# Block transposes on VectorE and a trip through DRAM in place of TensorE transposes, in a gated linear attention followed by a feed-forward layer

## The chip, the cores and the metric

The kernel runs on one core of one Trainium2 chip. A core has a matrix engine (TensorE, PE in the profile), three engines for elementwise work (VectorE or DVE, ScalarE or ACT, GpSimd or POOL) and SyncE (SP), which here issues nearly all DMA transfers. Each engine has a queue of instructions of its own, which it works through in order, and they wait for each other by semaphores. The metric is the device time of one execution in microseconds (us), lower is better.

## What is computed

Two layers. The first is a recurrence with a complex gate for each of 4 batches and 8 heads, over 768 steps, with head size 48. The second is a feed-forward layer over all 3072 tokens, 384 to 2048 to 384.

```python
mag = np.sqrt(a_re * a_re + a_im * a_im)
scale = np.minimum(mag, 0.999) / (mag + 1e-06)
a_re_n, a_im_n = (a_re * scale, a_im * scale)
for t in range(S):
    new_re = ar * S_re - ai * S_im
    new_im = ar * S_im + ai * S_re
    S_re, S_im = (new_re + k[t] outer v[t], new_im)
    y[:, :, t] = q[t] @ S_re
x = y.transpose(0, 2, 1, 3).reshape(B * S, H * D)
h = x @ w_in
sp = np.maximum(h, 0.0) + np.log1p(np.exp(-np.abs(h)))
out = (h * erf(sp)) @ w_out
```

Activations are float32; the two weight matrices come in as 64-bit words and are narrowed in the kernel.

## The kernel before

**Units and chunks.** The 3072 tokens are cut into 12 units of 256 tokens, three units to a batch; a unit has two chunks of 128 tokens. The recurrence is done a chunk at a time: gates are turned into a decay `pr` and an angle (cosine and sine, `CS`), keys and queries are multiplied with both, and then a chunk is a masked product of queries and keys, plus the contribution of the state S that the chunks before have left.

**The steps of a chunk** (function `chunk`, lines 981 to 1067), in order:

- `prep` (L977, L992), VectorE: `kr` or `qr` = key or query times decay, then `kt` or `qt` = that times cosine and sine. `kt` and `qt` have 128 tokens as partitions and 8 heads x 96 numbers along the row.
- `cols` (L1001, L1004): the score product needs the 96 numbers as partitions, so TensorE transposes `kt` and `qt` head by head into PSUM (4 heads to a tile `tr`, 4 tiles a chunk), and ScalarE or VectorE copies each tile into `kT` or `qT`. Keys are copied by ScalarE; the queries by ScalarE before unit 3 and by VectorE from unit 3 on (`qact` in `WHEN`); the very first chunk does it the other way about for keys.
- `state` (L1024, L1033, L1035): `kt` times `v`, added to the old state, times the decay over the chunk (`w`, a row of `pr` that goes to DRAM and comes back as a column, L967 and L970).
- `scores` (L1012, L1015): for each head `kT` as weights, `qT` as columns; VectorE multiplies with the triangle and leaves `A`.
- `xT` (L1060, L1064): `A` with `v`, and `qT` with the state, in blocks of 32 output partitions, into one PSUM tile; ScalarE copies it into `xT`. The first chunk of a batch has no part with the state.

A float32 product is two matmul instructions in the profile, a transpose is one.

**The feed-forward part.** `ff_in` (L1080, L1082) multiplies `xT` with `w_in`, eight row blocks of 128 to a slab, two slabs a unit. `softplus` and `erf_times_h` (L726, L1108 to L1111) put each slab through ScalarE and VectorE. `ff_out_8` (L1140) and, for units 3 to 10, `ff_out_7` (L1178, with sums on VectorE at L1125, L1126, L1192, L1195) multiply with `w_out`; the result leaves by L1150 and L1211.

**Order.** Every step of every unit has a place on one line of time, counted in units: the table `WHEN` and lines 1300 to 1342. All steps are sorted by it (L1360), and a scheduling layer turns this order into the queues of the engines. A chunk's steps stand at its begin plus the offsets `st`. Gates of a unit are done well ahead (`gr`, or `gate` for units 2 and 3): `g_mag`, `g_tan`, `g_log`, `g_turn`, `g_angle`, `g_decay`, `g_sin`. Keys, queries and values of a unit are loaded 0.38 units ahead (L1325).

**Waits on transfers.** SP's queue holds loads, the decay rows, output stores and, in `g_angle` from unit 3 on, a row that carries the angle from one chunk to the next (L931), for which VectorE waits at L932. Each issue waits in SP's order.

**Buffers.** `kt`, `qt`, `z` and `yy` have one buffer, `kT` two, `qT` three. `T["s"]`, `T["y"]` are scratch tiles of the gates, `lr` the log of the decay; the row of L931 lands in `s`.

Of the kernel before, what the change touches and what calls it, by code (L numbers as in the profile page):

```python
# [10 lines left out]
FP = mybir.dt.float32  # L11
# [5 lines left out]
OP = mybir.AluOpType  # L17
PSUM = bass.MemoryType.PSUM

P = 128  # L20
# [15 lines left out]
def weave(*streams):  # L36
# [5 lines left out]
    for _, _, _, step in sorted(order, key=lambda e: e[:3]):  # L42
# [1 line left out]

WHEN = {'qact': 3,
 'a00': [0.385, 0.699, 0.3, 0.31, 0.32, 0.33, 0.569, 0.34, 0.35, 0.63],
 'a01': [0.526, 0.422, 0.611, 0.637, 0.649, 0.542, 0.659, 0.66, 0.67, 0.681],
 'n': [0.676, 0.782, 0.769, 0.972, 1.105, 1.183, 1.312, 1.472, 1.61, 1.914, 1.96, 2.139, 2.151, 2.632, 2.395],  # L50
 'g1': [0.702, 0.752, 0.792, 0.802, 0.835, 0.842, 0.873],
 'att': {1: [[0.931, 1.297], 1.089], 2: [[1.716, 2.133], 1.029], 3: [[3.038, 3.627], 1.205]},
 'gate': {2: [1.212, 1.259, 1.372, 1.391, 1.423, 1.442, 1.362], 3: [1.508, 1.606, 1.912, 2.106, 2.59, 2.234, 2.172]},
 'hps': {0: [[0.767, 0.876], [1.01, 1.426]],
         1: [[1.778, 2.017], [2.342, 2.684]],
         2: [[3.136, 3.262], [3.538, 3.868]],
         11: [[11.97, 12.371], [12.438, 12.72]]},
 'act': {0: [2.6, 2.924],
         1: [3.328, 3.7],
         2: [4.148, 4.4],  # L60
         3: [4.9, 5.2],
         4: [5.752, 6.098],
         10: [11.679, 12.031],
         11: [12.456, 12.882]},
 'ops': {0: [3.021, 3.377, 3.704],
         1: [4.001, 4.639, 4.84],
         2: [4.452, 4.798, 4.884],
# [1 line left out]
         10: [12.146, 12.41, 13.01],  # L69
         11: [12.97, 13.469, 14.216]},  # L70
 'T': 5.125,
 'gr': [-1.569, -1.419, -1.119, -0.953, -0.478, -0.129, -1.279],
 'st': [0.014, 0.03, 0.059, 0.09, 0.12, 0.15, 0.206, 0.25, 0.281, 0.388],
 'hr': [1.113, 1.509, 1.573, 1.938],
 'ar': [1.472, 1.947],
 'or': [2.163, 2.683, 3.173],
# [4 lines left out]
 'rest': 12.3,  # L81
 'ok': 13.7,
 'al': [[11.145, 11.515], [11.266, 11.738]],
 'qone': 0,
 'c1g': [0.36, 0.37, 0.38],
 'warm': 0.335}

# [526 lines left out]
def quotient_path(  # L614
# [62 lines left out]
    make_identity(nc, ident)  # L677
    triu = const.tile([P, P], FP, name="triu")
    make_upper_triangular(nc, triu, val=1.0, diag=True)
    cold = tmp.tile([P, P], FP, tag="m", name="cold")  # L680
    vector.memset(cold, 0.0)
    ones = const.tile([P, 1], FP, name="ones")
    vector.memset(ones, 1.0)
# [193 lines left out]
    def g_(nm, u, cc):  # L877
        if cc[0] == 0:
            T[nm, u] = gat.tile([P, C, DM], FP, tag=nm, name=nm)
        return T[nm, u][:, cc[0]:cc[1]]  # L880
# [4 lines left out]
    def g_mag(u, cc=ALL):  # L885

        ar, ai = gate(u, cc)
        s, y = t_("s", cc), t_("y", cc)
        T["s", u] = T["s"]
        i = u * C + cc[0]  # L890
        T["kept"] = u == 1
        act(out=s, in_=ar, func=AF.Square, accum_out=large[:, i:i + 1])
        act(out=y, in_=ai, func=AF.Square)
        T["kept"] = False
        vector.tensor_tensor(out=s, in0=s, in1=y, op=OP.add)
# [14 lines left out]
    def g_log(u, cc=ALL):  # L910
        s, y = T["s"][:, cc[0]:cc[1]], T["y"][:, cc[0]:cc[1]]
        act(out=s, in_=s, func=AF.Ln)
        act(out=y, in_=s, func=AF.Exp, scale=-0.5)
        act(out=y, in_=y, func=AF.Ln, scale=EPS, bias=1.0)
        vector.tensor_scalar(out=s, in0=s, scalar1=0.5, scalar2=math.log(CAP), op0=OP.mult, op1=OP.min)
        T["logs"] = vector.tensor_tensor(out=g_("lr", u, cc), in0=s, in1=y, op=OP.subtract)

    def g_turn(u, cc=ALL):
        th = T["th", u][:, cc[0]:cc[1]]
# [2 lines left out]
    def g_angle(u, c):  # L922

        th = T["th", u][:, c, :]
        goes_on = u % PER > 0 or c > 0
        on_pe = u < PER
        if goes_on:
            prev = T["F", u][:, c - 1, :] if c > 0 else T["F", u - 1][:, C - 1, :]
            if not on_pe:
                row = T["s", u][0:1, c, :]  # L930
                nc.sync.dma_start(out=row, in_=prev[P - 1:P, :])  # L931
                vector.scalar_tensor_tensor(out=th[0:1, :], in0=row, scalar=TAU, in1=th[0:1, :],  # L932
                                               op0=OP.mult, op1=OP.add)
        ps = ps_b.tile([P, DM], FP, tag="b", name="sum")
        nc.tensor.matmul(out=ps, lhsT=turns, rhs=th, start=True, stop=not (goes_on and on_pe))
        if goes_on and on_pe:
            nc.tensor.matmul(out=ps, lhsT=ident[:, P - 1:P].to_broadcast([P, P]), rhs=prev, start=False, stop=True)
        F = g_("F", u, (c, c + 1))[:, 0, :]
        vector.tensor_scalar(out=F, in0=ps, scalar1=MAGIC, scalar2=MAGIC, op0=OP.add, op1=OP.subtract)
        vector.tensor_tensor(out=F, in0=ps, in1=F, op=OP.subtract)  # L940
# [40 lines left out]
    def chunk(u, c):  # L981
# [5 lines left out]
        def prep(nm, e):  # L987
# [5 lines left out]
                st[nm] = t  # L993
            return f

        def cols(nm, g):
            def f():
                pool, tag = (ps_h, "ff") if (nm, u, c) == ("q", 0, 0) else (ps_a, "a")
                ps = pool.tile([P, HG, P], FP, tag=tag, name="tr")
                for j in range(HG):  # L1000
                    nc.tensor.transpose(out=ps[0:D2, j, :], in_=st[nm][:, g * HG + j].rearrange("p u d -> p (u d)"),  # L1001
                                        identity=ident)
                t = att2.tile([P, HG, P], FP, tag=f"{nm}T", name=f"{nm}T", bufs=2 if nm == "k" else 3)
                (vector.tensor_copy if (nm == "k" if (u, c) == (0, 0) else nm == "q" and u >= WHEN["qact"] and g >= WHEN["qone"]) else scalar.copy)(out=t[0:D2], in_=ps[0:D2])  # L1004
                st[nm, g] = T["cols", nm, g] = t
            return f

        def scores(g):
            def f():
                ps = ps_a.tile([P, HG, P], FP, tag="a", name="sc")  # L1010
                for j in range(HG):
                    nc.tensor.matmul(out=ps[:, j, :], lhsT=st["k", g][0:D2, j, :], rhs=st["q", g][0:D2, j, :],  # L1012
                                     start=True, stop=True)
                A = att2.tile([P, HG, P], FP, tag="A", name="A")
                vector.tensor_tensor(out=A, in0=ps, in1=triu.unsqueeze(1).to_broadcast([P, HG, P]), op=OP.mult)  # L1015
                st["A", g] = A
            return f
# [20 lines left out]
        def xT():  # L1038

            if c == 0:  # L1040
                T["xT", u] = xp.tile([P, KD, NT], FP, tag="xT", name="xT")
            ps = ps_b.tile([P, KD, P], FP, tag="b", name="y")

            steps = [[] for _ in range(P // QUAD)]
            for i in range(KD):
                for b in range(P // QUAD):
                    pair, o = divmod((i * P + b * QUAD) // QUAD, 2 * D // QUAD)

                    parts = [(0, o * QUAD)] if o * QUAD < D else []
                    parts += [(1, o * QUAD + GAP)] if (o + 1) * QUAD > D else []  # L1050
                    todo = []
                    for e, lo in parts:
                        g, k_ = divmod(2 * pair + e, HG)
                        todo.append((T["v", u][:, c, pair, lo:lo + QUAD], st["A", g][:, k_, :]))
                        if not first:
                            todo.append((T["S"][0:D2, pair, lo:lo + QUAD], st["q", g][0:D2, k_, :]))
                    steps[b] += [(i, lhsT, rhs, n == 0, n == len(todo) - 1) for n, (lhsT, rhs) in enumerate(todo)]
            for turn in zip(*steps):
                for b, (i, lhsT, rhs, start, stop) in enumerate(turn):
                    nc.tensor.matmul(out=ps[b * QUAD:(b + 1) * QUAD, i, :], lhsT=lhsT, rhs=rhs,  # L1060
                                     start=start, stop=stop)
            if not last:
                T["S"] = st["S"]
            scalar.copy(out=T["xT", u][:, :, c * P:(c + 1) * P], in_=ps)  # L1064

        return [prep("k", 1), prep("q", 0), cols("k", 0), cols("k", 1), cols("q", 0), cols("q", 1), state, scores(0),
                scores(1), xT]

# [164 lines left out]
    def warm(n, t):  # L1233

        ps = ps_o.tile([P, DM], FP, tag="o", name="unread")
        for _ in range(n):
            tc.keep_in_program_order(nc.tensor.matmul(out=ps[:, 0:P], lhsT=t, rhs=t, start=True, stop=True))
# [60 lines left out]
        wt[j][0]()  # L1298

    plan = list(zip(WHEN["a00"][4:], first[4:])) + list(zip(WHEN["a01"], chunk(0, 1)))  # L1300
    plan += [(WHEN["warm"], lambda: warm(WARM[5], T["cols", "k", 1][0:D2, 0]))]
    plan += [(0.60, partial(load_qkv, 1))] + [(0.605, wt[j][0]) for j in (6, 7)]
    plan += [(WHEN["n"][j - 1], wt[j][1]) for j in range(2, 16)]
    plan += [(WHEN["n"][5] + 0.001 * j, wt[j][0]) for j in (8, 9)] + [(WHEN["n"][j - 1] + 0.001, wt[j + 2][0]) for j in range(8, 14)]
# [15 lines left out]
    for u in range(NU):  # L1320
        if u > 0:
            begins, spread = WHEN["att"].get(u, ((u, u + WHEN["c1"]), 1.0))
            for c in range(C):
                plan += [(begins[c] + p * spread, f) for p, f in zip(STEPS, chunk(u, c))]
            plan += [(u - 0.38, partial(load_qkv, u))] if u > 1 else []  # L1325
        if u > 1:
            mag, log, turn, angle, decay, sin, get = WHEN["gate"].get(
                u, [u + x for x in WHEN["gr"]])
# [86 lines left out]
```

## Time and profile before

| | |
|---|---|
| device time, median of 3 runs | 723.15 us (721.3 to 723.63) |
| span of the profiled execution | 719.8 us |
| TensorE busy | 699.2 us |
| ScalarE busy | 590.1 us |
| VectorE busy | 577.8 us |
| DMA bytes | 54.50 MB, mean 76 GB/s |
| DMA packets under 512 bytes | 142612 of 156012 |

The span runs from the first to the last instruction of one execution; the device time of a run is a little longer. A busy share is the time in which at least one instruction of the engine was under way. Rows of groups give: line, engine, operation, result and inputs, shapes, count, then busy us and the mean duration of one in ns, then idle time of the engine ahead of these instructions and what ended it. Two larger groups which stand beside the change:

```profile
L725 ACT ACT_TABLE_LOAD x90 | 115.5, 1283 | 1.4
L1080 PE MATMUL hps<-xT,w_in_sb 128*128 128x256 f32 x1152 | 270.6, 381 | 2.1 <-ACT xT L1064 1.4
```

The first is ScalarE changing its function table, the second the first feed-forward product. A table of stages gives, for each stretch of the run, the busy us of each engine with the number of instructions, then TensorE's granted clock, DMA's share and GB/s.

### The profile page before, as it was taken

To read this page: it belongs to the slowest core of one execution; us is meant where nothing else is said; L and a number is where in the kernel's file an instruction comes from. 1 tells how busy PE (TensorE), PEld (TensorE's weight loads), DVE (VectorE), ACT (ScalarE), POOL (GpSimd) and SP (SyncE) were. 2 spreads that over 40 slices of the span, in tenths; PEclk is the share of its full clock that TensorE was granted. 3 is DMA by queue.
4 is the path that set the end of the run, shared out by engine and by line. 5 is a ranking of instruction groups with operands and counts; after the bars stand their busy time and mean duration, and the time that the engine had idled before them with its cause. 6 is when DMAs were issued, how large, how long until landed. Compare 5 with 4: busy or idle time off the path is not lost.

```text
span 719.8 us, 12612 instructions
## 1 busy us (share of the span) xinstructions
PE 699.2 (97%) x5048; PEld 595.8 (83%) x5048; DVE 577.8 (80%) x1001; ACT 590.1 (82%) x767; POOL 1.1 (0%) x8
## 2 busy tenths in 40 slices
PE   9899999899999999999999999999999999999996
PEld 8778788767777678988988988997898799899985
DVE  6868985877598789979799799799799896776562
ACT  7879969979988998799699799798797797656860
POOL 0000000000000000000000000000000000000000
PEclk9999999999999999999999999999999999999999
DMA  9886874021302312503233233233331500200000
GB/s 216 222 186 131 200 202 100 1 45 34 56 8 50 66 34 53 136 24 67 87 68 67 88 56 73 94 56 67 99 78 45 132 2 22 89 1 23 0 24 27
DMA packets 156012, 54.50 MB, mean 76 GB/s; under 512 B 142612, under 2 KB 145704, under 8 KB 155944
## 3 DMA queue, kind: packets, MB, share of 16 engines
q1 hardware_dynamic: 153864, 53.22, 31.6%
q8 instruction: 41, 0.67, 0.4%
q10 hardware_dynamic: 2080, 0.39, 0.3%
q14 instruction: 27, 0.22, 0.1%
HBM read 48.82 MB, written 4.75 MB: 74 GB/s over the span
## 4 chain that ended last, share of the span: by engine, by line
ACT 37%; PE 29%; DVE 26%; DMA 5%; issue 3%; SPq 0%; ACTq 0%
PE hps L1080 10%; ACT L725 8%; ACT yy L726 8%; ACT z L726 8%; PE ops L1140 4%; DVE z L1108 4%; DVE yy L1109 4%; DVE e L1110 4%; DVE h L1111 3%; PE ops L1178 3%; ACT e L726 3%; DMA again<-in_moe_w_out_dram 2%; PE tr L1001 2%; PE sc L1012 2%; ACT h L1082 2%
## 5 line engine op out<-in xcount | busy, mean ns | idle before, releaser
L1080 PE MATMUL hps<-xT,w_in_sb 128*128 128x256 f32 x1152 | 270.6, 381 | 2.1 <-ACT xT L1064 1.4
L1080 PEld LDWEIGHTS hps<-xT,w_in_sb 128*128 128x128 f32 x1152 | 212.8, 190 | 36.3 <-ACT xT L1064 2.6
L725 ACT ACT_TABLE_LOAD x90 | 115.5, 1283 | 1.4
L1108 DVE TENSOR_TENSOR z<-z,yy 128x512 f32<-128x512 f32 x96 | 62.9, 684 | 41.0 <-ACT e L726 40.6
L726 ACT ACTIVATE e<-z 128x512 f32<-128x512 f32 x96 | 57.6, 626 | 32.4 <-DVE h L1111 32.0
L1082 ACT COPY h<-hps 128x512 f32<-128x512 f32 x96 | 55.1, 576 | 35.0 <-PE hps L1080 34.8
L1140 PE MATMUL ops<-w_out_sb,h 128*128 128x384 f32 x224 | 77.0, 488 | 0.6 <-DVE h L1111 0.4
L1178 PE MATMUL ops<-w_out_sb,h 128*128 128x192 f32 x384 | 70.9, 327 | 0.1
L1178 PEld LDWEIGHTS ops<-w_out_sb,h 128*128 128x128 f32 x384 | 63.7, 190 | 1.8 <-DVE o L1189 0.5
L1140 PEld LDWEIGHTS ops<-w_out_sb,h 128*128 128x128 f32 x224 | 41.6, 190 | 26.7 <-DVE h L1111 1.5
L1109 DVE SCALAR_TENSOR_TENSOR yy<-z,yy 128x512 f32<-128x512 f32 x96 | 62.8, 682 | 0.4
L1110 DVE TENSOR_TENSOR e<-e,yy 128x512 f32<-128x512 f32 x96 | 62.7, 681 | 0.2
L1111 DVE SCALAR_TENSOR_TENSOR h<-e,h 128x512 f32<-128x512 f32 x96 | 62.7, 681 | 0.2
L726 ACT ACTIVATE z<-h 128x2048 f32<-128x2048 f32 x24 | 45.9, 1912 | 15.2 <-DVE seen L774 11.4
L1012 PE MATMUL sc<-qT,kT 96*128 96x128 f32 x384 | 51.0, 279 | 0.6 <-DVE qT L1004 0.3
L1012 PEld LDWEIGHTS sc<-qT,kT 96*128 96x128 f32 x384 | 47.4, 192 | 4.2 <-DVE qT L1004 1.6
L1178 PE MATMUL ops<-T,S 128*128 128x192 f32 x256 | 47.7, 328 | 0.0
L726 ACT ACTIVATE yy<-z 128x2048 f32<-128x2048 f32 x24 | 45.9, 1912 | 0.4
L726 ACT ACTIVATE z<-z 128x2048 f32<-128x2048 f32 x24 | 45.9, 1911 | 0.4
L726 ACT ACTIVATE yy<-yy 128x2048 f32<-128x2048 f32 x24 | 45.9, 1912 | 0.3
L1178 PEld LDWEIGHTS ops<-T,S 128*128 128x128 f32 x256 | 42.1, 190 | 2.6 <-DVE S L1192 0.3
L1015 DVE TENSOR_TENSOR A<-sc,triu 128x512 f32<-128x512 f32 x48 | 32.4, 682 | 11.9 <-PE sc L1012 11.4
(129 smaller groups left out, 1043.4 us busy)
## 6 DMA issues: line engine op xcount, KB each, us to landing
raw<-in_moe_w_in_dram SPq DMA_DIRECT2D x8, 768.0 KB
raw<-in_moe_w_out_dram SPq DMA_DIRECT2D x8, 768.0 KB
again<-in_moe_w_in_dram SPq DMA_DIRECT2D x8, 768.0 KB
ar<-in_a_re_dram SPq DMA_DIRECT2D x24, 192.0 KB
k<-in_k_dram SPq DMA_DIRECT2D x24, 192.0 KB
q<-in_q_dram SPq DMA_DIRECT2D x24, 192.0 KB
v<-in_v_dram SPq DMA_DIRECT2D x48, 96.0 KB
out_dram<-o SPq DMA_DIRECT2D x24, 192.0 KB
```

What stands on the lines that cost most here:

```text
L725: in_order(scalar.preload_act_table_set(sets[0]))
L726: in_order(scalar.activation(func=func, **kw))
L1012: nc.tensor.matmul(out=ps[:, j, :], lhsT=st["k", g][0:D2, j, :], rhs=st["q", g][0:D2, j, :], start=True, stop=True)
L1015: vector.tensor_tensor(out=A, in0=ps, in1=triu.unsqueeze(1).to_broadcast([P, HG, P]), op=OP.mult)
L1080: nc.tensor.matmul(out=ps[:, e, :], lhsT=w_in_sb[:, kd, f0:f0 + P], rhs=T["xT", u][:, kd, :], start=(kd == 0), stop=(kd == KD - 1))
L1082: scalar.copy(out=T["h", u, sl][:, i:i + 2, :], in_=ps)
L1108: vector.tensor_tensor(out=z, in0=z, in1=y, op=OP.mult)
L1109: vector.scalar_tensor_tensor(out=y, in0=z, scalar=-2.0, in1=y, op0=OP.add, op1=OP.mult)
L1110: vector.tensor_tensor(out=e, in0=e, in1=y, op=OP.mult)
L1111: vector.scalar_tensor_tensor(out=h, in0=e, scalar=1.0 / RT2, in1=h, op0=OP.add, op1=OP.mult)
L1140: nc.tensor.matmul(out=ps, lhsT=lhsT, rhs=w_out_sb[:, i, :], start=i == HALF, stop=i == KF - 1)
L1178: ins = nc.tensor.matmul(out=ps, lhsT=a(sl)[:, i], rhs=b(sl, i), start=sl == 0 and i == 0, stop=sl == NSL - 1 and i == HALF - 1)
```

## The change

From the second unit on (unit 1; both chunks) a chunk has no `cols` any more. VectorE transposes `kt` and `qt` in blocks of 32 by 32 into a tile `X`; the blocks then have to change places across partitions, which goes by way of DRAM: one DMA writes `X` into a DRAM tile `turned` (768 KB), three DMAs read it back, one for each block of 32 rows, into a tile `KQ`. `KQ` holds the columns of keys and queries of all heads with the head as the innermost index (16 numbers), so that one head's columns stand 16 numbers, 64 bytes, apart. The score and output products read it so, in all units; unit 0 still transposes on TensorE and copies its tiles into `KQ`. `KQ` and `X` have one buffer.

The first four steps of a chunk (two `prep`, two `turn`) stand 0.14 units (unit 1, first chunk: 0.08) ahead of the chunk's begin; keys, queries and values are loaded 0.6 units ahead in place of 0.38; some gate steps are sooner. The log of the decay stays in `s` (tile `lr` is gone), and the row that carries the angle lands in `y`.

```diff
- 'gr': [-1.569, -1.419, -1.119, -0.953, -0.478, -0.129, -1.279],
- 'st': [0.014, 0.03, 0.059, 0.09, 0.12, 0.15, 0.206, 0.25, 0.281, 0.388],
+ 'gr': [-1.443, -1.419, -1.119, -0.953, -0.6, -0.27, -1.279],
+ 'st': [0.206, 0.25, 0.281, 0.388],
+ 'lead': {0: -0.14, (1, 0): -0.08},
+ 'turn': [0.0, 0.015, 0.02, 0.03],
+ 'lq': -0.6,
...
-        T["logs"] = vector.tensor_tensor(out=g_("lr", u, cc), in0=s, in1=y, op=OP.subtract)
+        vector.tensor_tensor(out=s, in0=s, in1=y, op=OP.subtract)
...
-                row = T["s", u][0:1, c, :]
+                row = T["y", u][0:1, c, :]
...
+        def columns():
+            T["KQ"] = st["KQ"] = att2.tile([P, P, 2 * H], FP, tag="KQ", name="KQ", bufs=1)
+
...
-                t = att2.tile([P, HG, P], FP, tag=f"{nm}T", name=f"{nm}T", bufs=2 if nm == "k" else 3)
-                (vector.tensor_copy if (nm == "k" if (u, c) == (0, 0) else nm == "q" and u >= WHEN["qact"] and g >= WHEN["qone"]) else scalar.copy)(out=t[0:D2], in_=ps[0:D2])
-                st[nm, g] = T["cols", nm, g] = t
+                i = "kq".index(nm) * H + g * HG
+                t = st["KQ"][0:D2, :, i:i + HG].rearrange("p t h -> p h t")
+                (vector.tensor_copy if nm == "k" and c == 0 else scalar.copy)(out=t, in_=ps[0:D2])
...
+        def turn(nm):
+
+            def f():
+                if nm == "k":
+                    T["X"] = att1.tile([P, D2 // QUAD, QUAD, 2 * H], FP, tag="X", name="X")
+                src = st[nm].rearrange("p h u d -> p h (u d)").rearrange("p h (b d) -> p b h d", d=QUAD)
+                i = "kq".index(nm) * H
+                vector.transpose(out=T["X"][:, :, :, i:i + H].rearrange("p b t h -> p b h t"), in_=src)
+                if nm == "k":
+                    return
+                columns()
+                D_ = dram.tile([P, D2 // QUAD, QUAD * 2 * H], FP, tag="turned", name="turned", bufs=2)
+                nc.sync.dma_start(out=D_, in_=T["X"].rearrange("p b t h -> p b (t h)"))
+                for b in range(D2 // QUAD):
+                    nc.sync.dma_start(out=st["KQ"][b * QUAD:(b + 1) * QUAD].rearrange("p (i t) h -> p i (t h)", t=QUAD),
+                                      in_=D_[:, b].rearrange("(i f) x -> f i x", f=QUAD))
+            return f
+
+        def head(nm, h):
+            return st["KQ"][0:D2, :, "kq".index(nm) * H + h]
...
-                    nc.tensor.matmul(out=ps[:, j, :], lhsT=st["k", g][0:D2, j, :], rhs=st["q", g][0:D2, j, :],
+                    nc.tensor.matmul(out=ps[:, j, :], lhsT=head("k", g * HG + j), rhs=head("q", g * HG + j),
...
-                            todo.append((T["S"][0:D2, pair, lo:lo + QUAD], st["q", g][0:D2, k_, :]))
+                            todo.append((T["S"][0:D2, pair, lo:lo + QUAD], head("q", 2 * pair + e)))
...
+        if u > 0:
+            return [prep("k", 1), prep("q", 0), turn("k"), turn("q"), state, scores(0), scores(1), xT]
...
-                plan += [(begins[c] + p * spread, f) for p, f in zip(STEPS, chunk(u, c))]
-            plan += [(u - 0.38, partial(load_qkv, u))] if u > 1 else []
+                lead = WHEN["lead"].get((u, c), WHEN["lead"][0])
+                at_ = [begins[c] + lead + p for p in WHEN["turn"]] + [begins[c] + p * spread for p in STEPS]
+                plan += list(zip(at_, chunk(u, c)))
+            plan += [(u + WHEN["lq"], partial(load_qkv, u))] if u > 1 else []
```

## The prediction

> **What bounds the kernel now.** First the totals of the page, then the busy time by stage of the run, because an average over the run hides where an engine is full.
>
> ```profile
> span 719.8 us, 12612 instructions
> PE 699.2 (97%) x5048; PEld 595.8 (83%) x5048; DVE 577.8 (80%) x1001; ACT 590.1 (82%) x767; POOL 1.1 (0%) x8
> ...
> DMA  9886874021302312503233233233331500200000
> ```
> ```profile
> core 0: us, PE busy (x) PEld busy (x) DVE busy (x) ACT busy (x) POOL busy (x), PEclk, DMA share, GB/s
> 0.00:60.00 60.00, 55.23 (x424) 47.48 (x425) 43.23 (x86) 48.52 (x94) 1.08 (x8) 1.00 0.87 192
> 60.00:120.00 60.00, 58.55 (x540) 48.36 (x539) 54.64 (x82) 51.23 (x76) 0.00 (x0) 1.00 0.76 183
> 120.00:240.00 120.00, 117.33 (x682) 86.51 (x682) 87.77 (x148) 107.67 (x133) 0.00 (x0) 1.00 0.18 33
> 240.00:560.00 320.00, 315.80 (x2377) 276.78 (x2379) 283.10 (x491) 282.70 (x352) 0.00 (x0) 1.00 0.30 70
> 560.00:720.00 160.00, 152.34 (x1042) 136.70 (x1030) 109.10 (x197) 99.97 (x116) 0.00 (x0) 0.99 0.12 36
> ```
>
> TensorE is at 98 to 99% of every stage but the first and the last, at full clock: it is the bound. But from 240 to 560 us VectorE is at 283.1 of 320 (88%) and ScalarE at the same, so neither is far behind. DMA is busy only in the first 120 us. In the chain of waits ScalarE holds 37%, TensorE 29% and VectorE 26%: an engine that never idles is rarely a releaser, so I trust the busy times more than this split.
>
> A busy record of a matmul overlaps the next one, so its mean duration is not its price. The price is the distance of starts in the timeline:
>
> ```profile
> 401.72 1.04 PE L1001 MATMUL tr<-ident,qt 128*96 128x128 f32 x8
> 402.59 0.49 PE L1178 MATMUL ops<-T,S 128*128 128x192 f32 x2
> ...
> 406.38 1.95 PE L1012 MATMUL sc<-qT,kT 96*128 96x128 f32 x16
> 408.17 1.47 PE L1178 MATMUL ops<-T,S 128*128 128x192 f32 x8
> ```
>
> Eight transposes take 402.59 - 401.72 = 0.87 us, 109 ns each (not the 275 ns of the group's mean); sixteen score matmuls 1.79 us, 112 ns each. The groups of the operations concerned:
>
> ```profile
> L1001 PE MATMUL tr<-ident,qt 128*96 128x128 f32 x192 | 27.1, 275 | 2.3 <-DVE qt L992 1.2 <-ACT kT L1004 1.0
> L1001 PE MATMUL tr<-ident,kt 128*96 128x128 f32 x192 | 26.1, 275 | 4.4 <-DVE kt L992 4.1
> L1012 PE MATMUL sc<-qT,kT 96*128 96x128 f32 x384 | 51.0, 279 | 0.6 <-DVE qT L1004 0.3 <-ACT qT L1004 0.2
> L1060 PE MATMUL y<-qT,S 96*32 96x128 f32 x640 | 33.8, 272 | 0.0
> ```
> ```profile
> L1004 DVE COPY qT<-tr 96x512 f32<-96x512 f32 x36 | 24.1, 679 | 2.1 <-PE tr L1001 1.9
> L992 DVE TENSOR_TENSOR qt<-qr,CS 128x768 f32<-128x768 f32 x23 | 21.8, 948 | 0.1
> ```
> ```profile
> L1004 ACT COPY kT<-tr 96x512 f32<-96x512 f32 x46 | 24.9, 574 | 5.0 <-PE tr L1001 4.9
> ```
>
> **What the Trainium skill says.** "VectorE: DVE Perf Modes", section The three transpose paths: VectorE transposes only within 32 by 32 blocks, 311 ns for a 128x128 bf16 grid; so somebody must move the blocks, here DMA. No run yet shows a float32 one. "SBUF — State Buffer", section Door 1: The DMA port swizzle: lines of 16 bytes, an access that goes to a new line each time pays a penalty (no size given), and a DMA into partitions 0..31 reaches 8 of 16 ports, 189 GB/s at 1 MiB. Nothing in this trace steps 16 bytes or more per element, so it can't confirm either. "DMA: Bandwidth & Descriptors", section Anatomy of one DMA: about 2 us fixed plus the bytes. The trace agrees: the chain shows 1.91 us for a 192 KB output store.
>
> **The change part by part.** Units 1 to 11 have 22 chunks of 128 tokens, with 16 transposes each.
>
> Removed, TensorE: 22 x 16 = 352 transposes x 109 ns = 38.4 us, 1.74 us a chunk. Removed, ScalarE: 58 copies become 6, 52 x 0.576 = 29.9 us, and the built order has 7 table loads fewer (86 for 93), 7 x 1.283 = 9 us. ScalarE goes to about 551 us and is out of the question as a new bound. Removed, VectorE: 36 copies x 0.679 = 24.4 us, 1.36 us a chunk from unit 3 on.
>
> Added, VectorE: 44 block transposes of 768 elements a partition. Nearest row: an operation of 768 elements, 0.948 us, the low end. They write with a step of 16 elements, 64 bytes, so each element is on a new line; if that halves the stream, it costs the stream once more: the 384-element products of the same page take 0.546 us, so 384 elements more take 0.40 us and 768 take 0.80 us, 1.75 us in all, the high end. I take 1.2 us, nearer the low end: the penalty is stated without size, and a VectorE element every 1.05 ns leaves a line more time than a column of TensorE does. VectorE then has 577.8 - 24.4 + 44 x 1.2 = 606 us; ends 595 and 630.
>
> Added, strided reads: every score matmul (both operands) and the q part of the output matmuls now read with a step of 64 bytes. Today these take 384 x 0.112 = 43 us and 640 x 0.0275 = 17.6 us (eight in 0.22 us in the timeline). Low end: nothing. In the timeline twelve `hps` matmuls of 256 columns take 2.59 us, so a float32 column takes 0.84 ns; for a 2-byte operand "TensorE: Matmul & The Clock Gate", section Back-to-back issue gap, gives N/2.4 ns, 0.42 ns a column (no such operand is in this trace). A line thus has twice the time here. High end: doubled, +60.6 us. A gain is excluded, the same columns pass. I take nothing.
>
> Added, DMA: per chunk one write of 768 KB and three reads of 256 KB. The write: 1.91 us + (768-192) KB at the 386 GB/s which the busiest slice of the DMA view of 60 to 130 us reached = 3.4 us. The reads: 2 us + 768 KB at 189 to 386 GB/s = 4 to 6 us. SP waits for the write to land, and for the previous chunk's last output matmul (KQ has one buffer), and all that is behind it waits too: the row for the running angle, output stores, loads. In the built order of the changed program, priced with the distances above, 14 to 28 us of TensorE work lie between what a read waits for on TensorE and its first score in most chunks; only in the chunks up to unit 5 are there five with 6 to 10. So the reads are hidden after unit 5, and partly not before 130 us, where DMA is already 66 to 87% busy: I charge 4 us. If the cover were gone everywhere, 22 x 5 us = 110 us.
>
> Moved: gates, keys and queries are prepared up to 0.14 unit sooner; the same instructions, no new ones. Angle logs now reuse their input's buffer; no time of its own. Unit 0's copies write with a step, 8 copies, at most 8 x 0.6 = 5 us of engines with room at that time: nothing.
>
> **The sum by stage** (against 719.8). The transposes in each stage are counted from the trace: 6 chunks up to 120 us (2 of them unit 0), 4 to 240, 11 to 560, 3 after.
> - 0 to 120: 4 x 1.74 = -7.0, reads in a busy DMA +4: -3.
> - 120 to 240: 4 x 1.74 = -7.0; VectorE has room (88 of 120); one microsecond lost to new waits: -6.
> - 240 to 560: 11 x 1.74 = -19.2 would leave 300.8 us. VectorE needs 283.1 - 11 x 1.36 + 22 x 1.2 = 294.5 us. With other waits it won't run above some 96% over such a stage (its fullest 20 us are 99%): 294.5 / 0.96 = 307. So -13. VectorE becomes the bound here, and what is late next is h for the second product.
> - After 560: -5.2, the tail's dependent chain keeps 1: -4.
> Together -26: 694 of span. Runs stand 723.15 - 719.8 = 3.35 above it: 697.
>
> **Rivals.**
> 1. All goes through: the transposes cost 0.95 us, VectorE needs 268.1 + 20.9 = 289 of 301: -38 + 4 = 686 of span, 689 with the offset; to 684 without the early loss. For it: TensorE's 99%. Against: VectorE at 96%.
> 2. Slow block transposes, 1.75 us: 268.1 + 38.5 = 306.6 / 0.96 = 319, stage three gains 1, stage two 4, the rest 6: about 709 of span, 712; up to 722 if waits on VectorE pile up. For it: the 64-byte step.
> 3. The other side: the strided operands. At doubled price +60.6 - 38.4 + 5 = +27, 747 of span, 750; it decides from 26/60.6, a 43% slower read, upward. For it: each element on its own line, for weights and columns both. Against: the 0.84 ns that a float32 column takes anyway.
> 4. The round trip by way of SP's one queue is late in each chunk: from 26/22 = 1.2 us more a chunk it eats the gain, at 2 us a chunk 694 + 44 = 738, 741. For it: in the waits of SP's queue one output store holds it for 41 us today; against: the 14 us of cover.
>
> **How the numbers follow.** The main case 0.47 (690 to 708), rival 1 0.10, rival 2 0.14 (three quarters of it faster), rival 3 0.20, rival 4 0.09. A measurement can tell about 0.3%, 2.2 us, from no change. Faster: 0.47 + 0.10 + 0.11 = 0.68. Same 0.05: rests of rivals 2 and 3. Slower 0.27. The range goes from 684 to 740: below lie the best of rival 1, above the doubled reads, together under 0.2. The main case's own is 690 to 708.
>
> **What would show it.** Right: no transposes after unit 0; TensorE's busy sum 38 lower; block transposes near 1.2 us; score starts still 112 ns apart; VectorE above 92% in the middle with TensorE now idling before the second product. Wrong: scores 150 ns or more apart (rival 3); scores waiting for the DMA into KQ after 150 us (rival 4); block transposes at 1.7 us or more (rival 2).

## The result, and the profile after

The changed kernel takes 806.79 us (median of 5 runs, 805.07 to 811.48), the kernel before 722.15 us beside it: a ratio of 1.1179, 95% interval 1.1146 to 1.1212. It is 12% slower, outside the range given. The profiled execution has a span of 809.7 us. Totals of the page:

```profile
PE 742.7 (92%) x4696; PEld 626.4 (77%) x4696; DVE 615.2 (76%) x1009; ACT 561.9 (69%) x708; POOL 1.1 (0%) x8
...
PE   9896959789879999969999998999996999999997
...
PEclk9797959899989999999999999899998999999999
DMA  9765945971231534255553362373561660520000
```

TensorE has 352 matmul records fewer, the removed transposes, and yet is busy 43.5 us longer. It is also idle 809.7 - 742.7 = 67.0 us, against 20.6 before, and its mean granted clock is 0.949 against 0.998: in the last rows, which cut the span into 40 slices and give tenths, the clock digits below 9 stand in or just behind slices in which TensorE stands still for some microseconds. VectorE is busy 76% of the span, less than before as a share. So two things have happened: each of some TensorE instructions got dearer, and TensorE waits. The table of stages (columns as before) says where it waits:

```profile
core 0: us, PE busy (x) PEld busy (x) DVE busy (x) ACT busy (x) POOL busy (x), PEclk, DMA share, GB/s
0.00:60.00 60.00, 55.64 (x376) 48.22 (x377) 37.92 (x76) 43.59 (x82) 1.08 (x8) 0.89 0.83 185
60.00:120.00 60.00, 41.42 (x271) 32.34 (x270) 45.23 (x66) 31.89 (x45) 0.00 (x0) 0.77 0.63 152
120.00:240.00 120.00, 102.72 (x574) 78.16 (x576) 79.95 (x117) 82.82 (x102) 0.00 (x0) 0.94 0.55 117
240.00:560.00 320.00, 306.29 (x1972) 257.48 (x1968) 266.99 (x436) 248.42 (x302) 0.00 (x0) 0.97 0.44 107
...
```

More than half of the idle time lies between 60 and 240 us, 18.6 and 17.3 us in two stages. From 240 to 560 us VectorE is at 267 of 320 (83%), nowhere near the 96% that the forecast had it at.

The groups of the operations concerned show what got dearer:

```profile
L1035 PE MATMUL sc<-KQ 96*128 96x128 f32 x384 | 88.5, 395 | 2.6 <-DMA KQ<-turned 2.6
L1035 PEld LDWEIGHTS sc<-KQ 96*128 96x128 f32 x384 | 86.2, 307 | 5.4 <-issue 3.9
L1083 PE MATMUL y<-KQ,S 96*32 96x128 f32 x640 | 56.1, 403 | 0.0
L1017 DVE STREAM_TRANSPOSE X<-kt 128x768 f32<-128x768 f32 x22 | 32.7, 1487 | 0.0
L1007 ACT COPY KQ<-tr 96x512 f32<-96x512 f32 x6 | 5.9, 1046 | 1.2 <-PE tr L1003 1.2
```

All of them read or write with the step of 64 bytes. A record of a score product went from 279 to 395 ns, of a weight load from 192 to 307, of the query part of the output from 272 to 403, and the copy into `KQ` in unit 0 from 574 to 1046. The real price is again the distance of starts, at full clock in the timeline:

```profile
469.59 3.63 PE L1035 MATMUL sc<-KQ 96*128 96x128 f32 x16
...
473.04 0.83 PE L1203 MATMUL ops<-T,S 128*128 128x192 f32 x4
...
474.05 0.63 PE L1083 MATMUL y<-KQ,S 96*32 96x128 f32 x8
...
474.49 0.41 PE L1083 MATMUL y<-A,v 128*32 128x128 f32 x4
```

Sixteen score matmuls take 473.04 - 469.59 = 3.45 us, 216 ns each where it was 112. Eight of the query part of the output, whose columns alone are read with the step, take 0.44 us, 55 ns each where it was 27.5: the columns by themselves are enough to double the distance. The first group above has the answer about the trip through DRAM: in 384 score matmuls TensorE waited 2.6 us, once, for `KQ`.

What TensorE did wait for, over the whole run:

```profile
engine line waited for: us in total, times, longest us
PE y L1083 <- DVE A L1038: 14.9, 3, 8.8
PE hps L1105 <- DVE w_in_sb L800: 8.0, 3, 4.4
...
PE ops L1165 <- DVE h L1136: 5.5, 2, 5.2
...
```

The longest line of the same view of the kernel before is 4.1 us, transposes that wait for the keys:

```profile
PE tr L1001 <- DVE kt L992: 4.1, 6, 1.7
```

What a releaser stands behind in its own queue can be seen for the longest wait, 8.8 us. The timeline of VectorE up to its end:

```profile
103.71 0.96 DVE L899 TENSOR_TENSOR th<-th,ai 128x768 f32<-128x768 f32 x1 [4.17 <-ACT th L723]
...
106.51 0.95 DVE L989 TENSOR_TENSOR kt<-kr,CS 128x768 f32<-128x768 f32 x1
...
107.84 1.46 DVE L1017 STREAM_TRANSPOSE X<-kt 128x768 f32<-128x768 f32 x1
109.17 0.92 DVE L989 TENSOR_TENSOR qt<-qr,CS 128x768 f32<-128x768 f32 x1
110.02 0.67 DVE L1038 TENSOR_TENSOR A<-sc,triu 128x512 f32<-128x512 f32 x1
...
110.74 0.66 PE L1083 MATMUL y<-A,v 128*32 128x128 f32 x8 [8.77 <-DVE A L1038]
```

`A`, 0.67 us of work for which TensorE stands still, comes after gates that wait 4.17 us for ScalarE, then after the next chunk's preparation and its block transpose. The scores that `A` needs were done at 101.97 us (110.74 - 8.77) at the latest, in the middle of those 4.17 us, in which VectorE had nothing else to do. From 60 to 120 us VectorE is busy 45.2 of 60: it is not full here, its order is wrong for TensorE.

### The profile page after: what moved, and what is told of

It is laid out like the page before. It is cut to its first block, busy times and chain, and to the rows that moved or that the text cites. A ratio compares the mean times of both kernels' runs of the same rounds, so it can differ in the third digit from the quotient of the medians.

```text
span 809.7 us, 11964 instructions
## 1 busy us (share of the span) xinstructions
PE 742.7 (92%) x4696; PEld 626.4 (77%) x4696; DVE 615.2 (76%) x1009; ACT 561.9 (69%) x708; POOL 1.1 (0%) x8
## 2 busy tenths in 40 slices
DMA packets 168682, 89.08 MB, mean 110 GB/s; under 512 B 144020, under 2 KB 147112, under 8 KB 168616
## 4 chain that ended last, share of the span: by engine, by line
PE 67%; ACT 17%; DVE 10%; DMA 3%; issue 2%; SPq 0%; DVEq 0%; ACTq 0%
PE hps L1105 23%; PE ops L1203 12%; PE ops L1165 9%; PE sc L1035 9%; PE y L1083 6%; ACT L722 4%; PE kv L1047 3%; ACT yy L723 2%; ACT z L723 2%; PE sum L932 2%; PE sum L949 2%; DMA KQ<-turned 2%; ACT th L723 1%; ACT e L723 1%; DVE X L1017 1%
## 5 line engine op out<-in xcount | busy, mean ns | idle before, releaser
L1105 PEld LDWEIGHTS hps<-xT,w_in_sb 128*128 128x128 f32 x1152 | 220.0, 194 | 56.1 <-ACT h L1107 7.4
L1035 PE MATMUL sc<-KQ 96*128 96x128 f32 x384 | 88.5, 395 | 2.6 <-DMA KQ<-turned 2.6
L1035 PEld LDWEIGHTS sc<-KQ 96*128 96x128 f32 x384 | 86.2, 307 | 5.4 <-issue 3.9
L1083 PE MATMUL y<-A,v 128*32 128x128 f32 x768 | 50.7, 308 | 20.6 <-DVE A L1038 14.9
L1165 PEld LDWEIGHTS ops<-w_out_sb,h 128*128 128x128 f32 x224 | 43.5, 197 | 33.5 <-DVE h L1136 6.1
L1203 PEld LDWEIGHTS ops<-w_out_sb,h 128*128 128x128 f32 x384 | 64.8, 192 | 3.7 <-DVE o L1214 1.1
L1083 PEld LDWEIGHTS y<-A,v 128*32 128x32 f32 x768 | 30.0, 126 | 39.5 <-DVE A L1038 18.4
L1203 PE MATMUL ops<-T,S 128*128 128x192 f32 x256 | 50.8, 340 | 6.7 <-DVE S L1150 4.9
L1083 PE MATMUL y<-KQ,S 96*32 96x128 f32 x640 | 56.1, 403 | 0.0
L1203 PEld LDWEIGHTS ops<-T,S 128*128 128x128 f32 x256 | 45.2, 199 | 9.8 <-DVE S L1150 5.4
```

Source lines behind the costliest of these rows:

```text
L1035: nc.tensor.matmul(out=ps[:, j, :], lhsT=head("k", g * HG + j), rhs=head("q", g * HG + j), start=True, stop=True)
L1105: nc.tensor.matmul(out=ps[:, e, :], lhsT=w_in_sb[:, kd, f0:f0 + P], rhs=T["xT", u][:, kd, :], start=(kd == 0), stop=(kd == KD - 1))
L1165: nc.tensor.matmul(out=ps, lhsT=lhsT, rhs=w_out_sb[:, i, :], start=i == HALF, stop=i == KF - 1)
L1203: ins = nc.tensor.matmul(out=ps, lhsT=a(sl)[:, i], rhs=b(sl, i), start=sl == 0 and i == 0, stop=sl == NSL - 1 and i == HALF - 1)
```

## The experiments

Each time stands beside the kernel before, run on the same chip: 721.31, 722.37, 721.63 or 721.65 us. The letters of the theories are those of the expectations. The scheduling layer makes the order of the instructions anew for each kernel. In the traces the pair of experiment 1 has one and the same sequence on TensorE, VectorE, ScalarE and SP. In the comparisons of 2 to 8 the sequences differ widely, so a difference of times there holds the price of another order too: of VectorE's sequence about 0.7 agrees between `sooner` and `trip_unread`, 0.8 between `quad` and the changed kernel, 0.4 between `flat` and the changed kernel.

**1. The step of 64 bytes by itself** (`pe_strided`), and the same tile without it (`pe_flat1`). Both are the kernel before with its transposes on TensorE; keys and queries go into one `KQ` tile, with the head innermost in the first and the token innermost in the second.

```diff
 # pe_strided
+ T["KQ"] = st["KQ"] = att2.tile([P, P, 2 * H], FP, tag="KQ", name="KQ", bufs=KQB)
+ t = st["KQ"][0:D2, :, i:i + HG].rearrange("p t h -> p h t")
+ return st["KQ"][0:D2, :, "kq".index(nm) * H + h]
 # pe_flat1, against pe_strided
- T["KQ"] = st["KQ"] = att2.tile([P, P, 2 * H], FP, tag="KQ", name="KQ", bufs=KQB)
+ T["KQ"] = st["KQ"] = att2.tile([P, 2 * H, P], FP, tag="KQ", name="KQ", bufs=KQB)
- t = st["KQ"][0:D2, :, i:i + HG].rearrange("p t h -> p h t")
+ t = st["KQ"][0:D2, i:i + HG]
- return st["KQ"][0:D2, :, "kq".index(nm) * H + h]
+ return st["KQ"][0:D2, "kq".index(nm) * H + h]
```

> The kernel before, still transposing on TensorE, but its copies go into one tile KQ laid out as in the changed kernel, so that score and output products read with a step of 64 bytes; no block transposes, no DRAM, no earlier times. Theory S (the strided reads double the price of the score products and of the q part of the output products, and that is most of the loss): sc 216 ns apart in place of 112, +40 and +17 us of TensorE work, 775 to 800 us. Theory O (the earlier places put the score masks of VectorE behind the next chunk's preparation, TensorE idles): 722 to 735. Theory D (DMA round trips and traffic hold things up): 722 to 735.

> The control of the run before: the same one tile KQ with one buffer, but each head's 128 columns contiguous. All theories: 720 to 728 us; what it is above 722 is the price of the one buffer. Against it the strided twin shows the step alone.

Measured: 779.93 us with the step (1.0834, 1.0792 to 1.0876), 720.87 us without (0.9997, 0.9983 to 1.0011). The groups of `pe_strided`:

```profile
L1018 PE MATMUL sc<-KQ 96*128 96x128 f32 x384 | 92.5, 400 | 1.6 <-ACT KQ L1008 1.4
L1008 ACT COPY KQ<-tr 96x512 f32<-96x512 f32 x58 | 57.8, 1055 | 8.9 <-PE tr L1004 8.8
L1066 PE MATMUL y<-KQ,S 96*32 96x128 f32 x640 | 52.8, 399 | 0.0
L1008 DVE COPY KQ<-tr 96x512 f32<-96x512 f32 x36 | 36.6, 1032 | 5.8 <-PE tr L1004 5.7
```

and those of `pe_flat1`:

```profile
L1018 PE MATMUL sc<-KQ 96*128 96x128 f32 x384 | 51.1, 279 | 0.7 <-DVE KQ L1008 0.3 <-ACT KQ L1008 0.3
L1066 PE MATMUL y<-KQ,S 96*32 96x128 f32 x640 | 33.8, 272 | 0.0
L1008 ACT COPY KQ<-tr 96x512 f32<-96x512 f32 x58 | 31.7, 575 | 5.6 <-PE tr L1004 5.4
L1008 DVE COPY KQ<-tr 96x512 f32<-96x512 f32 x36 | 24.2, 680 | 2.5 <-PE tr L1004 2.3
```

Both are as theory S and the control had it. The two have the same instructions in the same order; TensorE is 98% busy in the first and 97% in the second. The step alone costs 779.93 - 720.87 = 59 us where TensorE is the bound. The copies by ScalarE and VectorE got dearer too, which costs nothing visible here: TensorE is idle 18.5 us with the step and 21.3 without. The single buffer for keys and queries, which came with the change, costs nothing in this kernel.

**2. The earlier places by themselves** (`sooner`): the kernel before with the places of the change (the table `WHEN`), and nothing else of it.

```diff
- 'gr': [-1.569, -1.419, -1.119, -0.953, -0.478, -0.129, -1.279],
+ 'gr': [-1.443, -1.419, -1.119, -0.953, -0.6, -0.27, -1.279],
+ 'lead': {0: -0.14, (1, 0): -0.08},
+ 'lq': -0.6,
...
```

> The kernel before with only the earlier places of the change (gates, loads, the two preparations 0.14 units ahead), transposes on TensorE and contiguous reads kept. Theory S: 718 to 728 us. Theory O: 745 to 770, TensorE idling for VectorE's masks in the first 250 us. Theory D: 718 to 728.

Measured: 730.97 us (1.0149, 1.0118 to 1.0181), 10 us for a rearrangement that adds no instruction; it lies between the expectations, some 3 us above that of S and D. TensorE's busy time from 120 to 240 us falls from 117.3 to 114.0.

**3. The changed kernel without the lead** (`lead0`): the preparation begins at the chunk's own begin; gates and loads stay at their earlier places.

```diff
- 'lead': {0: -0.14, (1, 0): -0.08},
- 'turn': [0.0, 0.015, 0.02, 0.03],
+ 'lead': {0: 0.0},
+ 'turn': [0.014, 0.03, 0.035, 0.045],
```

> The changed kernel with the preparations and block transposes at the chunk's begin, in place of 0.14 (0.08) units ahead. If the earlier places are what hurts: 770 to 790. If the scores need them to have their columns in time (W): 830 or more, scores waiting for the DMA into KQ in most chunks.

Measured: 805.92 us (1.1153, 1.1108 to 1.1198), no different from the changed kernel, and neither expectation met. Scores now wait 9.1 us for `KQ`, once, in place of 2.6. How far ahead the preparation stands makes no difference to the whole.

**4. The trip on another queue** (`pool_queue`): the write and the three reads are issued by GpSimd.

```diff
- nc.sync.dma_start(out=D_, in_=T["X"].rearrange("p b t h -> p b (t h)"))
+ nc.gpsimd.dma_start(out=D_, in_=T["X"].rearrange("p b t h -> p b (t h)"))
...
- nc.sync.dma_start(out=st["KQ"][b * QUAD:(b + 1) * QUAD].rearrange("p (i t) h -> p i (t h)", t=QUAD),
+ nc.gpsimd.dma_start(out=st["KQ"][b * QUAD:(b + 1) * QUAD].rearrange("p (i t) h -> p i (t h)", t=QUAD),
```

> The changed kernel with only the four DMAs of the trip issued from GpSimd's queue, which is idle, in place of SP's. Theory Q in the form that SP's loads and rows stand behind the trip: 755 to 775, the waits of gates and rows go. Theory W: 800 to 812.

Measured: 806.23 us (1.1164, 1.1137 to 1.1192). This is theory W's figure: getting the trip out of SP's queue brings nothing in the whole, and TensorE still waits 14.5 us for `A`.

**5. Everything added, nothing of it used** (`trip_unread`): the changed kernel with transposes on TensorE again, contiguous `KQ`; `X` is still written with the step; block transposes, the write and the reads run at their places, but the reads go to a DRAM tile that nobody reads.

```diff
+ E_ = dram.tile([P, P // QUAD, QUAD * 2 * H], FP, tag="unread", name="unread", bufs=1)
...
- nc.sync.dma_start(out=st["KQ"][b * QUAD:(b + 1) * QUAD].rearrange("p (i t) h -> p i (t h)", t=QUAD),
+ nc.sync.dma_start(out=E_[b * QUAD:(b + 1) * QUAD],
...
- return [prep("k", 1), prep("q", 0), turn("k"), turn("q"), state, scores(0), scores(1), xT]
+ return [prep("k", 1), prep("q", 0), turn("k"), turn("q"), cols("k", 0), cols("k", 1), cols("q", 0), cols("q", 1), state, scores(0), scores(1), xT]
```

> The changed kernel with its earlier places, but TensorE transposes keys and queries as before (one contiguous tile KQ) and the products read those; the block transposes and the DRAM trip are still done on the same queue, and the three reads land in a DRAM tile that nobody reads. Sooner alone measured 731. If the trip costs by what it puts on VectorE, on SP's queue and on the DMA engines (theory Q): 765 to 790. If it costs by making the scores wait or by the order that follows from it (theory W): 733 to 748, the 44 block transposes of 1.49 us on an engine with room.

Measured: 773.18 us (1.0694, 1.0657 to 1.073), as theory Q had it and 42 us above `sooner`, with no consumer of the result. So the added work, with the order that it brings, costs without anybody waiting for what it makes. The profiled executions, 772.7 and 729.2 us, show two parts: the same 5048 matmul instructions leave TensorE idle 31.3 us longer, and they keep it busy 12.2 us longer, at a mean granted clock of 0.965 in place of 0.989. The longest wait is in the timeline of this run, SP's issues with the work around:

```profile
119.37 0.34 SPq L1022 DMA_DIRECT2D turned<-X  x1
...
120.23 0.55 DVE L937 TENSOR_TENSOR F<-sum,F 128x384 f32<-128x384 f32 x1
...
127.30 0.37 SPq L778 DMA_DIRECT2D raw<-in_moe_w_out_dram  x1
127.72 1.81 SPq L1024 DMA_DIRECT2D unread<-turned  x3
...
129.57 0.60 SPq L928 DMA_DIRECT2D y<-F  x1
...
134.19 0.55 DVE L929 SCALAR_TENSOR_TENSOR th<-y,th 1x384 f32<-1x384 f32 x1 [4.24 <-DMA y<-F]
134.79 1.65 PE L932 MATMUL sum<-th,turns 128*128 128x384 f32 x2 [9.93 <-DVE th L929]
```

The running angle `F` is there at 120.78 us. Its row is issued only at 129.57, since SP first waits 7.5 us with a load of weights for a buffer that VectorE has still to empty (`w_out_sb`, L800), and then issues the three reads in 1.8 us. TensorE stands for 9.93 us. Most of this delay is thus a load that the kernel before has too; the trip's own share of it is the 1.8 us.

**6. Each half of the added work** (`turn_only`: no DMAs; `trip_only`: no block transposes, the DMAs carry a tile of zeros in which each chunk renews 16 numbers a partition).

```diff
 # turn_only, against trip_unread
- nc.sync.dma_start(out=D_, in_=T["X"].rearrange("p b t h -> p b (t h)"))
- for b in range(D2 // QUAD):
-     nc.sync.dma_start(out=E_[b * QUAD:(b + 1) * QUAD],
-                       in_=D_[:, b].rearrange("(i f) x -> f i x", f=QUAD))
 # trip_only, against trip_unread
+ vector.tensor_scalar(out=T["X"][:, 0, 0, :], in0=st["k"][:, 0, 0, 0:2 * H], scalar1=1.0, scalar2=None, op0=OP.mult)
- vector.transpose(out=T["X"][:, :, :, i:i + H].rearrange("p b t h -> p b h t"), in_=src)
```

> The run trip_unread without its DMAs: the 44 block transposes of 1.49 us remain, nobody reads X. trip_unread took 773 and sooner without both 731. If the 65 us of VectorE work cost those 42 us (theory V): 760 to 775. If the DMAs do (theory M): 731 to 742.

> The run trip_unread without its block transposes: a constant tile, of which 16 numbers a partition are renewed in each chunk, makes the same DRAM trip at the same places. Theory V: 731 to 740. Theory M: 760 to 775. Both a half: 745 to 755.

Measured: 754.6 us (1.0456, 1.0424 to 1.0487) and 756.23 us (1.0497, 1.0442 to 1.0552): 24 and 25 us over `sooner`, about equal, and together a little more than both at once. The first lies between the two theories, the second just above the "both a half". In the first the longest wait of TensorE is 6.2 us for `A`, in the second 10.1 us for the row of the angle, behind the same load as in 5. That one half works by VectorE's order and the other by SP's is a guess from these two waits; 34.6 MB more through the DMA engines (89.08 for 54.50 in the changed kernel) and the new order of everything are not ruled out.

**7. Without the step, another layout of the trip** (`flat`, and `flat_pool` with its DMAs on GpSimd's queue): `KQ` with the token innermost, four writes and three reads, runs of 128 bytes.

```diff
- D_ = dram.tile([P, D2 // QUAD, QUAD * 2 * H], FP, tag="turned", name="turned", bufs=2)
+ D_ = dram.tile([QUAD, D2 // QUAD * 2 * H, P // QUAD, QUAD], FP, tag="turned", name="turned", bufs=2)
...
+ for i in range(P // QUAD):
+     nc.sync.dma_start(out=D_[:, :, i], in_=T["X"][i * QUAD:(i + 1) * QUAD].rearrange("p b h t -> p (b h) t"))
```

> The changed kernel with block transposes and DRAM trip kept, but no step anywhere: X is written contiguously, the DRAM tile is laid out so that each head comes back as 128 contiguous columns (four writes with runs of 128 bytes, three reads of 8 KB a partition). Theory S: sc 112 ns apart, block transposes 0.95 us, TensorE work 57 us less than in the changed kernel: 695 to 725 us. Theory O: the idle time stays, 735 to 760. Theory D: 790 or more, since the round trip gets no shorter.

> The run flat with its seven DMAs a chunk on GpSimd's queue. Its TensorE work is 38 us under that of the kernel before; if its 929 us come from SP's queue (Q): 690 to 760; if from late columns or from the order (W): 850 or more.

Measured: 929.26 us (1.2894, 1.2868 to 1.2919) and 869.51 us (1.203, 1.2002 to 1.2057). Theories S, O and, for the second, Q are missed by far; only the open ends are met (D's "790 or more", W's "850 or more"), which named no such size. In `flat` TensorE is busy 720 of 927 us; 77.7 us of its idle time wait for `h`. The scheduling layer also put the whole program in another order, so this pair says nothing of the step; its own price is seen in 1. Another queue brings 60 us here and nothing in 4. Why `flat` came out so slow stays open.

**8. Without the step, the same trip** (`quad`): inside `KQ` the order is block of 32 tokens, head, token. A run in DRAM stays as long, 2 KB, and one head's columns are runs of 32 numbers. A score product becomes four matmuls of 32 keys each, so that each reads its weights in one run; they write to four blocks of output partitions.

```diff
- T["KQ"] = st["KQ"] = att2.tile([P, P, 2 * H], FP, tag="KQ", name="KQ", bufs=1)
+ T["KQ"] = st["KQ"] = att2.tile([P, P // QUAD, 2 * H, QUAD], FP, tag="KQ", name="KQ", bufs=1)
...
- vector.transpose(out=T["X"][:, :, :, i:i + H].rearrange("p b t h -> p b h t"), in_=src)
+ vector.transpose(out=T["X"][:, :, i:i + H], in_=src)
...
+ for i in range(P // QUAD):
+     nc.tensor.matmul(out=ps[i * QUAD:(i + 1) * QUAD, j, :].rearrange("p (i t) -> p i t", t=QUAD),
+                      lhsT=head("k", g * HG + j)[:, i], rhs=head("q", g * HG + j), start=True, stop=True)
```

> The changed kernel with X and KQ laid out by blocks of 32 tokens (block, head, token), so that the DMAs keep their runs of 2 KB, the block transposes write contiguously, and every product reads runs of 32; the score product of a head is done as four matmuls with 32 weights columns each, which work beside each other as those of the output product do. Against the changed kernel TensorE has 57 us less to do, VectorE 24 us less. If the strided reads are the larger part of the loss (S): 735 to 760. If the rest of the change costs as it did in trip_unread, it stays above 722 by the 42 us less the 38 of the transposes: the same range's low half. A gain on the kernel before would need both gone: under 715.

Measured: 766.63 us (1.0631, 1.0597 to 1.0665), 40 us less than the changed kernel and 7 us above the expected range. Two of its groups:

```profile
L1036 PE MATMUL sc<-KQ 96*32 96x128 f32 x1536 | 50.2, 280 | 2.8 <-DMA KQ<-turned 2.8
L1017 DVE STREAM_TRANSPOSE X<-kt 128x768 f32<-128x768 f32 x22 | 21.3, 969 | 0.0
```

Four times as many score matmuls are busy for 50.2 us, as little as the 384 of before, and the block transpose takes 969 ns. So two things went here, the step in TensorE's reads and the step in VectorE's writes. The rest of the loss is waiting: TensorE is busy 692.2 of 761.3 us, 7 us less than before the change, and idle 69.1.

**9. The replacement from unit 3 on alone** (`quad_u3`): `quad`, with the chunks of units 1 and 2 on TensorE's transposes and at their old places.

```diff
- if u > 0:
+ if u > 2:
      return [prep("k", 1), prep("q", 0), turn("k"), turn("q"), state, scores(0), scores(1), xT]
...
+ if u < 3:
+     at_ = [begins[c] + p for p in (0.014, 0.03)] + [begins[c] + p * spread for p in [0.059, 0.09, 0.12, 0.15] + STEPS]
```

> The kernel of the run quad, in which keys and queries are contiguous runs of 32 and each score product is four matmuls, but with the block transposes, the trip and the earlier preparation only from unit 3 on: units 1 and 2 are transposed on TensorE as before (8 us of TensorE work more than in quad). Theory E, what the replacement costs beyond the strides is lost in the early stage, where chunks stand close to what they wait for: 740 us or less, 0 to 240 us as busy as before (TensorE above 55 us in each of the first two stretches of 60 and above 114 in 120 to 240), nothing lost later. Theory L, VectorE and the trip cost in every chunk alike: about 18 of the 22 chunks still pay, 755 to 770 us, with TensorE idle spread over 240 to 720 us too.

Measured: 742.98 us (1.0305, 1.0288 to 1.0322). Putting 64 transposes back made it 24 us faster. Its stages:

```profile
0.00:60.00 60.00, 55.36 (x542) 46.40 (x543) 44.93 (x89) 48.69 (x95) 1.09 (x8) 1.00 0.88 194
60.00:120.00 60.00, 58.41 (x709) 47.01 (x708) 50.63 (x79) 47.44 (x73) 0.00 (x0) 1.00 0.69 167
120.00:240.00 120.00, 108.38 (x732) 76.62 (x731) 89.37 (x144) 101.68 (x120) 0.00 (x0) 0.97 0.40 89
240.00:560.00 320.00, 299.65 (x2627) 254.26 (x2626) 270.25 (x458) 256.60 (x315) 0.00 (x0) 0.96 0.47 116
```

The first 120 us are as full as before. From 240 to 560 us TensorE is idle 20.4 us (before 4.2), with VectorE and ScalarE at 84% and 80%. The time lies between the two expectations: units 1 and 2, four of the 22 chunks, carry 24 of the 45 us that `quad` loses, although their 64 transposes are TensorE work again, so theory E holds for about half, though from 120 to 240 us TensorE is at 108.4 and not above 114; and the other 18 chunks still lose, as theory L says, though less each than these four. No version that was run is faster than the kernel before.

## Why the prediction was wrong

A ladder of runs leads from the old kernel to the new one: 721.6, earlier places +9.4 (`sooner`), block transposes and trip with nobody waiting +42.2 (`trip_unread`), TensorE's transposes out, the trip's result used and block transposes without the step -6.6 (`quad`), the step of 64 bytes in reads and block transposes +40.2 (the changed kernel, 806.8). Each rung holds the change of order that came with it; only the pair of experiment 1 is free of that. The forecast's steps against it:

- **"Added, strided reads ... I take nothing": the step that failed.** The measurement is its own high end: 216 ns in place of 112, and 59 us (the pair of experiment 1) against the 60.6 worked out as the bound. The reason given for nothing was that a float32 column has twice the time for each line. It fell: 128 columns with the step take 216 ns, 1.69 ns each, where they took 0.875. The "twice" was weak already: the Trainium skill, "TensorE: Matmul & The Clock Gate", section Back-to-back issue gap, gives the formula used there for a matmul by itself, and about 81 ns for 128 columns in a stream of weight loads and matmuls, against which the 112 ns of this trace are 1.4 times, not twice. Of the penalty, the skill's "SBUF — State Buffer", section Door 1: The DMA port swizzle, says that it exists, without a size; the pair shows one. A bound known from both sides, with a plausible argument and no measurement, had been settled at its cheap end. The sign that the prediction gave for this case, scores 150 ns or more apart, was met. Between `quad` and the changed kernel the step costs 40 us, not 59, though there the block transposes have it too. Idle time is nearly the same in the two profiles (69.1 and 67.0 us), and the 64 matmuls of eight score products take only a little longer than the sixteen of before (1.89 us from start to start in the timeline of `quad`, 1.79 before), so where the other 19 us went stays open.
- **Removed, TensorE, -38.4 us: wrong as time.** From `trip_unread` to `quad`, where the block transposes lose their step as well, TensorE's busy sum falls by 716.4 - 692.2 = 24.2 us and the time by 6.6; TensorE's idle time grows (56.3 to 69.1 us). The sum by stage took nearly each microsecond of TensorE's work out of the span, which holds only as long as nothing else makes TensorE wait.
- **"Moved ... no new ones", charged nothing:** 9 to 10 us (`sooner`).
- **VectorE, 606 us:** 615.2 came out. The block transpose took 1.487 us where 1.2 was taken, 44 x 0.287 = 12.6 us more. Contiguous it takes 0.969, so the low end was right for the operation and the step costs 0.52 of the 0.80 that the high end gave it. But the claim that VectorE becomes the bound at 96% was wrong in kind: at 83% it already held TensorE up, which waits 14.9 us for `A`, 8.0 for weights and 5.5 for `h`. The two halves of 6 give the cost of the added work, 24 us for block transposes and 25 for the trip, where the sum had some 12 us for all of it (38.4 less 26), 4 of them for the trip. How much of it is the work, how much the traffic and how much the new order was not separated.
- **The trip's cover was right:** scores waited for `KQ` 2.6 us in all. Of its price, the write was low (it lands after 4.8 us, 3.4 forecast) and the reads about right (a single one lands after 4.2; 4 to 6 for the three). Rival 4, a trip that comes late, did not happen, and run 4 shows that SP's order alone isn't what makes the kernel slow.
- **ScalarE, 551 us:** 561.9, and no bound, as said; 7 table loads went, as worked out from the order.
- **Rival 3** named the mechanism and its price, and gave 750 us because it set that price against a gain of 38 us which did not come through, with 5 us for everything else where the runs show some 50. Rival 2's sign, block transposes of 1.7 us or more, was not met.

## What to carry to other kernels

A layout that makes a DMA's runs long can make every later read of TensorE pay: put a price on the step between neighbouring elements of a matmul's operands, and where none is known, measure it in a kernel that changes only the layout before deciding, and see in the trace that the order stayed. Work taken off an engine that was busy 98% hardly turned into time here, because others then kept it waiting; look at what stands in their queues ahead of the few short instructions that it waits for. And a change of places alone is worth a run by itself.

## What was not expected of the hardware

A step of 64 bytes in float32 made everything that was seen with it 1.5 to 2 times as long: a matmul with both operands so from 112 to 216 ns, one with only its columns so from 27.5 to 55 ns, a record of a weight load from 192 to 307 ns, a copy of 512 elements a partition out of PSUM from 575 to 1055 ns on ScalarE and from 680 to 1032 on VectorE, a block transpose of 768 elements from 969 to 1487 ns. A score product cut into matmuls of 32 weight columns, each to its own block of output partitions, costs nearly as little as with 128: 64 of them in 1.89 us against sixteen in 1.79. And in the long wait of the changed kernel the granted clock fell, to a mean of 0.57 from 100 to 120 us with TensorE busy 10.65 of 20 us, and it was still low when the work went on:

```profile
100.00:110.00 10.00, 1.97 (x10) 0.61 0.53 110
110.00:120.00 10.00, 8.68 (x86) 0.54 0.47 160
120.00:130.00 10.00, 10.00 (x48) 1.00 0.69 168
...
96.79 1.56 PE L1047 MATMUL kv<-v,kt 128*96 128x48 f32 x16 [0.60 <-DVE F L937]
...
112.19 2.80 PE L1047 MATMUL kv<-v,kt 128*96 128x48 f32 x16
```

The first three rows give TensorE's busy us, its clock, DMA's share and GB/s. The same sixteen matmuls take 1.56 us ahead of the wait and 2.80 just behind it, so part of the price of this wait was paid after it.
